# Tile 0's value products read v where it was loaded, in two halves of 64 rows; one stage's norms and copies change engines

## The chip, the cores and the metric

The kernel runs on one core of a Trainium2 chip. Its time is the device time of one launch in microseconds (us); what is shown is the median of several runs. The profile's engines are PE (TensorE, the matrix engine, with its weight loads as PEld), DVE (VectorE), ACT (ScalarE), POOL (GpSimd) and SP (SyncE, which only issues transfers here). Each engine takes its instructions in the order in which the program issued them to it; engines wait for one another through semaphores. Matrix products land in PSUM, which has eight banks of 512 fp32 columns on 128 partitions.

## What is computed

Sliding-window attention over 8 batches, 8 heads, 576 positions and 64 values a head, and then a two-layer network with the activation h cos(h) on all 4608 rows. `_attn_ref` and `_moe_ref` are these lines, with the constants filled in:

```python
scores = q @ k.T / 8                       # per batch and head, [576, 576]
rel = pos[:, None] - pos[None, :]
scores = where((rel >= 0) & (rel < 64), scores, -1e9)
attn = softmax(scores)
x = (attn @ v)  ->  [8 * 576, 512]         # heads side by side
h = x @ w_in                               # [4608, 2048]
out = (h * cos(h)) @ w_out                 # [4608, 512], fp32
```

## The kernel before, in words

**Attention.** A *unit* is 64 queries of one batch and one pair of heads (p = 0..3), against the at most 128 keys that they can see: their own block j of 64 keys and block j-1. The two heads of the pair lie on the two halves of the 128 partitions. Units go in groups of four (`GF`). For each group n: scores into one PSUM bank (`g_scores`), the row maxima on VectorE (`g_max`), exponentials with their row sums on ScalarE (`g_exp`, four instructions, each with a read of its accumulator), reciprocals on VectorE (`g_inv`), the product with them, called the norm here, on GpSimd or VectorE (`g_norm`, line 302), four transposes on TensorE into a bank of the rotating three named "t" (`g_trans`, line 311), and a copy out of it into `wT` on VectorE or ScalarE (`g_put`, through `copy`, line 109). `wT` has keys on its partitions: for odd j block j-1 on partitions 0 to 63 and block j on 64 to 127, for even j the other way round (`k_cols`, line 211).

**Values.** `load_v` (line 159) puts 128 rows of v of one batch into every second of eight slots: slot 2c has block 2c on its lower 64 partitions and block 2c+1 on the upper ones. Odd slots are filled by copies on the chip: `spread_v(0, 0)` copies lower halves of slots 2, 4, 6 to slots 1, 3, 5, `spread_v(0, 1)` copies upper halves of slots 0, 2, 4, 6 to slots 1, 3, 5, 7. Then slot j-1 has both blocks that unit j needs, each on the partitions on which `wT` has its keys, and one product on 128 rows per head and unit is enough (`values`, line 323: 16 products of 64 columns for a pair and a tile of 512 rows). `put_x` casts the bank to `xT`, which is what the network's first layer reads.

**The network.** Rows go in nine tiles of 512 (mt). A tile's first layer is 16 blocks (ff) of 4 products with w_in (line 351), one product for each pair of heads; a block's bank goes through a sine on ScalarE (line 519) and a product on VectorE (line 522) into `gT`; then 64 products with w_out (line 534). The attention of batch t+1 is woven into the network's tiles by a list of due times (`at`, `pump`).

**The first stage.** Tile 0 has nothing to be woven into. Its order is written out by hand in `FIRST`: each word is a step, and the order of the words is the order in which each engine gets its work. The words are: `tq.p`, `tk.p` (transposes of q, k of pair p), `pq.p.e`, `pk.p.e` (their copies out of PSUM on engine e: d VectorE, a ScalarE, p GpSimd), and, for pair p and group g of two, `s` scores, `m` maxima, `e` exponentials, `i` reciprocals, `n` norm, `w` transposes, `c` copy; `z` the two copies of `spread_v`, `v.p` values, `x.p` `put_x`; `l` the next of the loads on GpSimd's queue (w_in in three parts, batch 1's q and k rows, w_out in two parts); `tb` loads ScalarE's sine table. Products with w_in start before all four pairs are there: `h.p` issues the product of pair p for the first blocks (three of them), `hx.f` those of pairs 0 and 1 for block f, and `hl` those of pairs 2 and 3 for the first five blocks (`skew(0)` is 5). All later blocks get their four products in a row, in the tile's loop. Which bank a block uses is written in `H_FIRST`; the scores use the same five banks (`S_FIRST`), three other banks rotate as "t".

After `FIRST` GpSimd issues the last slot of batch 0's v (64 rows, block 8) and the five loads of batch 1's v.

Of the kernel before, what the change touches and what calls it, by code (L numbers as in the profile page):

```python
# [10 lines left out]
def _safe_warn(msg, *a, **kw):  # L11
# [14 lines left out]
GF = 4  # L26
# [25 lines left out]
def kernel(  # L52
# [43 lines left out]
    H_FIRST = ("O1", "X0", "X1", "S", "O0") * 3 + ("X0",)  # L96
# [69 lines left out]
    def spread_v(b, half, engine="p"):  # L166
        vt = values_of(b)
        to, of = ((vt[0:64, 1:7:2], vt[0:64, 2:8:2]), (vt[64:128, 1:8:2], vt[64:128, 0:7:2]))[half]
        if engine == "dma":
            nc.sync.dma_start(out=to, in_=of)  # L170
        else:
            copy(engine, to, of)

# [131 lines left out]

    def g_trans(n):
        w, u = st.pop(("w", n)), len(groups[n])
        if n in direct:
            st["tw", n] = t_ps = ps_t.tile([128, GF, 128], BF16, tag="t", name="tw_ps")
            for i in range(u):  # L310
                nc.tensor.transpose(t_ps[:, i], w[:, i], ident)  # L311
            return
        wT = att.tile([128, GF, 128], BF16, tag="wT", name="wT", bufs=20)
        nc.sync.dma_start(out=wT[:, 0:u], in_=w[:, 0:u].rearrange("p u c -> p (u c)"), transpose=True)
        st.update({("wT", unit): wT[:, i] for i, unit in enumerate(groups[n])})
# [18 lines left out]

    def put_x(mt, p, engine=None):
# [18 lines left out]
    def skew(mt):  # L354
        return 5 if mt < 2 else SKEW
# [6 lines left out]
    def skewed(mt, ks, n):  # L362
        for ff in range(skew(mt) if mt else SKEW):
# [110 lines left out]
    def load():  # L474
# [9 lines left out]
             "z": lambda half, engine=None: spread_v(0, half, engine),  # L484
# [3 lines left out]
             "c": lambda p, g, engine=None: g_put(2 * p + g, engine), "v": lambda p: values(0, p),  # L488
             "x": lambda p, engine=None: put_x(0, p, engine)}
# [3 lines left out]
    load_v(0, 4)  # L493
    for c in range(5):
# [82 lines left out]
```

## Time and profile before

| | before |
|---|---|
| median of 3 runs | 306.96 us (306.51 to 307.69) |
| the profiled execution's own time | 306.41 us |
| its span in the trace | 304.4 us |
| mean granted TensorE clock | 0.993 |
| busy: PE, PEld | 288.7 us (95%), 142.1 us (47%) |
| busy: DVE, ACT, POOL | 220.4 us (72%), 235.7 us (77%), 171.1 us (56%) |

How to read the lines shown below: a line of the timeline has the start in us from the span's start, the length in us, the engine, the line of the program, the operation, what it writes and reads, the shape, and how many instructions of the kind are merged in it (x4); a bracket at its end tells how long the engine stood idle before it and what ended that. The start of the next instruction of an engine can lie ahead of the end of the one before, as instructions overlap in the engine: what an instruction costs its engine is the distance from start to start. A line of the chain of waits has the start, the length and the piece of work. A line of a group has the busy time, the mean of one in ns, and the idle time before it.

### The profile page before, as it was taken

The page shows a single profiled execution, that of the slowest core. Times are in us where ns is not written, and L with a number is a line of the kernel's source. Part 1 is how long each engine was busy: PE and PEld are TensorE (multiplying, and loading weights), DVE is VectorE, ACT ScalarE, POOL GpSimd, SP SyncE. Part 2 cuts the span into 40 slices and gives each one's busy share as a digit, 9 for nine tenths or more (in the row PEclk, how much of TensorE's full clock was granted, in tenths as well). Part 3 has the DMA queues.
Part 4 walks back from the last instruction along what each step waited for, and adds up shares of the span by engine and source line. Part 5 has one row for each costly group of instructions (what it writes and reads, how often), then busy time and mean ns, then how long its engine had stood idle before and what let it go on. Part 6 is the DMA issues. An engine that isn't in the chain of part 4 may idle for free.

```text
span 304.4 us, 7847 instructions
## 1 busy us (share of the span) xinstructions
PE 288.7 (95%) x2628; PEld 142.1 (47%) x2668; DVE 220.4 (72%) x834; ACT 235.7 (77%) x786; POOL 171.1 (56%) x198
## 2 busy tenths in 40 slices
PE   3769999999999999999999999999999999999996
PEld 3544444544454445444544444444444454454443
DVE  3896889588787878787877787778778877236701
ACT  5997799967997799779987998799869986106600
POOL 8996257977774976497659665967433630000000
PEclk9989999999999999999999999999999999999999
DMA  7999999699969999999999979999994441011012
GB/s 150 181 211 207 207 155 139 105 165 191 225 114 155 225 164 132 154 201 183 138 167 208 189 106 172 157 219 123 180 172 110 87 130 62 0 72 70 0 69 71
DMA packets 165577, 43.88 MB, mean 144 GB/s; under 512 B 154720, under 2 KB 160800, under 8 KB 165536
## 3 DMA queue, kind: packets, MB, share of 16 engines
q0 software_dynamic: 99344, 18.06, 75.1%
q1 hardware_dynamic: 66048, 25.11, 40.2%
q8 instruction: 21, 0.34, 0.5%
q14 instruction: 20, 0.16, 0.2%
q10 hardware_dynamic: 144, 0.20, 0.2%
HBM read 36.70 MB, written 9.44 MB: 152 GB/s over the span
## 4 chain that ended last, share of the span: by engine, by line
PE 88%; DVE 6%; issue 2%; ACT 2%; DMA 1%; POOL 0%; DVEq 0%; POOLq 0%
PE h_ps L351 41%; PE out_ps L534 36%; PE o_ps L330 3%; PE s_ps L261 3%; DVE negm L273 1%; PE out_ps L371 1%; DMA first_f<-in_q_dram 1%; DVE w L302 1%; PE tq_ps L186 1%; DVE s L277 1%; DVE v L109 1%; PE tk_ps L186 1%; PE tw_ps L311 1%; PE s_ps L244 1%; ACT e L288 1%
## 5 line engine op out<-in xcount | busy, mean ns | idle before, releaser
L351 PE MATMUL h_ps<-xT,w_in 128*128 128x512 bf16 x556 | 127.1, 381 | 2.2 <-DVE xT L109 0.6
L534 PE MATMUL out_ps<-w_out,gT 128*128 128x512 bf16 x543 | 123.0, 379 | 1.8 <-issue 1.1
L522 DVE TENSOR_TENSOR gT<-h_ps,sin 128x512 bf16<-128x512 f32 x144 | 95.4, 688 | 33.6 <-ACT sin L519 33.4
L519 ACT ACTIVATE sin<-h_ps 128x512 f32<-128x512 f32 x144 | 82.9, 599 | 34.1 <-PE h_ps L351 32.8
L288 ACT ACTIVATE e<-s,negm 128x128 f32<-128x128 f32 x256 | 98.6, 388 | 0.3 <-DVE negm L277 0.3
L302 POOL TENSOR_TENSOR w<-e,rden 128x512 bf16<-128x512 f32 (+1 forms) x76 | 74.5, 993 | 31.5 <-DVE rden L295 29.1
L351 PEld LDWEIGHTS <-w_in 128*128 128x128 bf16 x576 | 56.0, 98 | 67.1 <-issue 2.7
L534 PEld LDWEIGHTS <-gT 128*128 128x128 bf16 x560 | 53.2, 98 | 62.4 <-issue 0.2
L277 DVE CUSTOM_DVE_ANT_0 s<-s_ps,mask 128x128 f32<-128x128 f32 x256 | 58.0, 284 | 0.1
L288 ACT ACTIVATION_READ_ACCUMULATOR e<-s,negm 128x1 f32 x256 | 48.1, 188 | 0.0
L149 POOL DMA_DIRECT2D rows<-in_q_dram x30 | 25.4, 867 | 25.9 <-DMA T<-rows 16.6
L162 POOL DMA_DIRECT2D v<-in_v_dram x35 | 29.8, 879 | 10.5 <-DMA rows<-in_k_dram 7.3
L109 ACT COPY out_sb<-out_ps 128x512 f32<-128x512 f32 (+1 forms) x18 | 10.1, 563 | 24.2 <-PE out_ps L534 18.7
L295 DVE RECIPROCAL rden<-den 128x4 f32<-128x4 f32 (+1 forms) x80 | 13.8, 172 | 19.2 <-ACT e L288 18.6
L149 POOL DMA_DIRECT2D rows<-in_k_dram x30 | 25.5, 897 | 2.2 <-DMA T<-rows 2.2
L109 DVE CAST xT<-o_ps 128x512 bf16<-128x512 f32 x27 | 17.6, 679 | 6.5 <-PE o_ps L330 6.3
L277 DVE DVE_READ_ACCUMULATOR2_ANT negm<- 128x1 f32 x256 | 21.2, 83 | 0.0
L109 DVE COPY out_sb<-out_ps 128x512 f32<-128x512 f32 x18 | 12.4, 689 | 12.0 <-PE out_ps L534 12.0
L288 ACT ACTIVATE e<-s_ps,negm 128x128 f32<-128x128 f32 x32 | 11.5, 425 | 1.6 <-DVE negm L273 1.6
L261 PE MATMUL s_ps<-T 64*64 64x128 bf16 x512 | 12.1, 221 | 0.0
L261 PEld LDWEIGHTS <-T 64*64 64x64 bf16 x512 | 8.2, 106 | 8.3 <-DVE negm L277 4.4
L330 PEld LDWEIGHTS <-v 128*64 128x64 bf16 x504 | 9.5, 112 | 4.3 <-issue 2.1
(56 smaller groups left out, 146.2 us busy)
## 6 DMA issues: line engine op xcount, KB each, us to landing
out_dram<-out_sb SPq DMA_DIRECT2D x16, 512.0 KB, 6.1
v<-in_v_dram POOLq DMA_DIRECT2D x28, 128.0 KB, 8.3
rows<-in_q_dram POOLq DMA_DIRECT2D x24, 128.0 KB, 5.2
rows<-in_k_dram POOLq DMA_DIRECT2D x24, 128.0 KB, 7.8
w_out<-in_moe_w_out_dram POOLq DMA_DIRECT2D x2, 1024.0 KB, 16.7
w_in<-in_moe_w_in_dram POOLq DMA_DIRECT2D x2, 768.0 KB, 12.4
wT<-w SPq DMA_TRANSPOSE x66, 3.9
out_dram<-out_sb SPq DMA_DIRECT2D x3, 256.0 KB, 2.0
```

The source lines that it names most:

```text
L109: {"a": nc.scalar.copy, "p": nc.gpsimd.tensor_copy}.get(engine, nc.vector.tensor_copy)(out, in_)
L149: nc.gpsimd.dma_start(out=rows(b)[lo:lo + n, slot * 512:slot * 512 + 512].rearrange("p (h d) -> p h d", h=H), in_={"q": q, "k": k}[name][b ...
L162: nc.gpsimd.dma_start(out=vt.rearrange("p (h d) -> p h d", h=H), in_=v[b, :, c * 128:c * 128 + n, :].rearrange("h p d -> p h d"))
L261: nc.tensor.matmul(out=s_ps[cross][to, u].rearrange("p (a t) -> p a t", a=2), lhsT=q_cols(b, p, j)[d], rhs=k_cols(b, p, j)[d], start=True, ...
L277: nc.vector.tensor_tensor_reduce(out=s[:, u], in0=s_ps[:, u], in1=mask[:, 2 - j % 2 if j else 0], scale=-scale if b else -1.0, scalar=BIG, ...
L288: nc.scalar.activation(e[:, u], s[:, u], AF.Exp, bias=negm[:, u:u + 1], scale=1.0 if n < n_first else -1.0, accum_out=den[:, u:u + 1])
L302: (nc.gpsimd if engine == "p" else nc.vector).tensor_tensor(out=w[:, 0:u], in0=e[:, 0:u], op=ALU.mult, in1=rden[:, 0:u].unsqueeze(2).to_br ...
L330: nc.tensor.matmul(out=o_ps[64 * h:64 * h + 64, 64 * i:64 * i + 64], lhsT=values_of(b)[:, max(j - 1, 0), 128 * p + 64 * h:128 * p + 64 * h ...
L351: nc.tensor.matmul(out=st["h", ff], lhsT=w_in_sb[:, ks, ff * 128:ff * 128 + 128], rhs=st["xT", mt][:, ks], start=start, stop=stop)
L519: nc.scalar.activation(sin, h_ps, AF.Sin, bias=math.pi / 2.0)
L522: nc.vector.tensor_tensor(out=gt[:, e], in0=h_ps, in1=sin, op=ALU.mult)
L534: nc.tensor.matmul(out=o_ps[e], lhsT=gT[ff // 2][:, ff % 2, ms * 128:ms * 128 + 128], rhs=w_out_sb[:, ff], start=ff == 0, stop=ff == n_ff - 1)
```

## The change

`spread_v` is no longer called for batch 0. Instead `values_first` reads v as it was loaded. For odd j the two blocks lie in one slot, on the partitions that `wT` wants: one product on 128 rows per head, as before. For even j the own block lies on the lower 64 partitions of slot j and block j-1 on the upper 64 of slot j-2: two products on 64 rows each, which add up in PSUM. They are issued in two steps, `va.p` (lower halves of even j, and odd j) and `vb.p` (upper halves), so a pair has 24 products and not 16. Pair 3 puts its upper halves into a bank of its own (`o2`) within `va.3`, and `put_x_last` (word `xl`) adds them: ScalarE copies `o2` to SBUF, VectorE copies the odd blocks and adds the even ones. The banks of `values_first` are X0, S and two of "t" (`O_FIRST`). One copy of 64 rows of the last slot remains for tile 1's unit of block 8 (`spread_last`, on GpSimd, behind the load of that slot).

Engines change: n.1.0 goes from VectorE to GpSimd; n.3.1 from VectorE to both, half each (`g_norm_halves`, word `nh`); pk.3, c.1.0 and c.2.0 from ScalarE to VectorE; c.3.0 and x.1 from VectorE to ScalarE; x.2 from ScalarE to VectorE. On GpSimd's queue the loads of batch 1's k rows and of w_out's first part move behind all norms. `tb` moves behind `xl`. `h.p` issues two blocks instead of three, `hx` only block 2, and `hl` the rest of three blocks instead of five.

```diff
 FIRST = (
     "tq.0 mk ck tk.0 pq.0.d pk.0.a s.0.1 tq.1 tk.1 l s.0.0 m.0.1 pq.1.d tq.2 e.0.1 pk.1.d s.1.0 pq.2.a "
-    "tk.2 s.1.1 i.0.1 tq.3 l m.0.0 m.1.0 pk.2.d n.0.1.p s.2.0 l w.0.1 tk.3 s.2.1 e.0.0 l e.1.0 m.1.1 "
-    "l i.0.0 e.1.1 pq.3.d i.1.0 m.2.0 pk.3.a e.2.0 n.0.0.p n.1.0.d z.1.p w.0.0 i.1.1 m.2.1 e.2.1 "
-    "s.3.0 s.3.1 c.0.1.d n.1.1.p c.0.0.d w.1.0 m.3.0 i.2.0 z.0.d c.1.0.a n.2.0.p w.1.1 c.1.1.d v.0 "
-    "i.2.1 v.1 n.2.1.p m.3.1 e.3.0 e.3.1 l x.0.d w.2.0 i.3.0 x.1.d h.0 c.2.0.a n.3.0.p w.2.1 h.1 hx.3 "
-    "i.3.1 n.3.1.d w.3.0 c.2.1.a w.3.1 tb v.2 c.3.0.d x.2.a c.3.1.d v.3 l x.3.d hx.4 hl "
+    "tk.2 s.1.1 i.0.1 tq.3 n.0.1.p l l m.0.0 m.1.0 pk.2.d s.2.0 w.0.1 tk.3 s.2.1 e.0.0 e.1.0 m.1.1 "
+    "i.0.0 n.0.0.p l e.1.1 pq.3.d i.1.0 n.1.0.p m.2.0 pk.3.d e.2.0 w.0.0 i.1.1 n.1.1.p m.2.1 e.2.1 "
+    "c.0.1.d s.3.0 s.3.1 i.2.0 n.2.0.p m.3.0 e.3.0 c.0.0.d w.1.0 va.0 i.2.1 n.2.1.p m.3.1 e.3.1 w.1.1 "
+    "c.1.0.d i.3.0 n.3.0.p c.1.1.d w.2.0 va.1 vb.0 w.2.1 c.2.0.d x.0.d i.3.1 nh.3.1 l l l c.2.1.a w.3.0 "
+    "c.3.0.a h.0 vb.1 x.1.a va.2 w.3.1 c.3.1.d va.3 vb.2 x.2.d h.1 hx.2 xl tb hl "
 )
...
-    H_FIRST = ("O1", "X0", "X1", "S", "O0") * 3 + ("X0",)
+    H_FIRST = ("O1", "X0", "O0", "S", "X1") * 2 + ("O1", "X0", "X1", "S", "O0", "X0")
+    O_FIRST = ("X0", "S", "t", "t")
...
+    def spread_last():
+        vt = values_of(0)
+        nc.gpsimd.tensor_copy(vt[64:128, 7], vt[64:128, 6])
...
+    def g_norm_halves(n):
+        (e, _), rden = st.pop(("e", n)), st.pop(("r", n))
+        w = att.tile([128, GF, 128], BF16, tag="w", name="w", bufs=8)
+        for engine, lo, hi in ((nc.vector, 0, 2), (nc.gpsimd, 2, 4)):
+            engine.tensor_tensor(out=w[:, lo:hi], in0=e[:, lo:hi], op=ALU.mult,
+                                 in1=rden[:, lo:hi].unsqueeze(2).to_broadcast([128, hi - lo, 128]))
+        st["w", n] = w
...
+    def values_first(p, part):
+        if part == "a":
+            st["o", 0, p] = bank(O_FIRST[p], "o_ps")
+        if p == PAIRS - 1:
+            st["o2"] = bank("X1", "o2_ps")[:, 0:MT // 2]
+        lower, upper, both = slice(0, 64), slice(64, 128), slice(0, 128)
+        parts = [(lower, j, j) for j in range(0, TU, 2)] + [(both, j - 1, j) for j in range(1, TU, 2)]
+        over = [(upper, max(j - 2, 0), j) for j in range(0, TU, 2)]
+        if part == "b":
+            parts = over
+        elif p == PAIRS - 1:
+            parts += over
+        for i, (ks, slot, j) in enumerate(parts):
+            apart = p == PAIRS - 1 and ks == upper
+            to = st["o2"][:, 32 * j:32 * j + 64] if apart else st["o", 0, p][:, 64 * j:64 * j + 64]
+            for h in range(2):
+                nc.tensor.matmul(out=to[64 * h:64 * h + 64], lhsT=vt_first(ks, slot, p, h),
+                                 rhs=st["wT", (0, p, j)][ks, 64 * h:64 * h + 64],
+                                 start=part == "a" and i == 0 or apart and j == 0, stop=True, skip_group_check=True)
...
+    def put_x_last():
+        p = PAIRS - 1
+        to, of = (x.rearrange("d (j o c) -> d o j c", o=2, c=64) for x in (st["xT", 0][:, p], st.pop(("o", 0, p))))
+        over = att.tile([128, GF, 128], F32, tag="s", name="over", bufs=4)[:, 0:2].rearrange("d a (j c) -> d (a j) c", c=64)
+        nc.scalar.copy(over, st["o2"].rearrange("d (j c) -> d j c", c=64))
+        nc.vector.tensor_copy(to[:, 1], of[:, 1])
+        nc.vector.tensor_tensor(out=to[:, 0], in0=of[:, 0], in1=over, op=ALU.add)
...
     def skew(mt):
-        return 5 if mt < 2 else SKEW
+        return 5 if mt == 1 else SKEW
...
     def skewed(mt, ks, n):
-        for ff in range(skew(mt) if mt else SKEW):
+        for ff in range(skew(mt) if mt else 2):
             first(mt, ff, ks, n == 0, n == PAIRS - 1)
...
     load_v(0, 4)
+    spread_last()
     for c in range(5):
         load_v(1, c)
```

More of the change, by code (lines that the diff above doesn't have):

```diff
@@ L332, in values, with vt_first @@
                                  rhs=wT[:, 64 * (h ^ cross):64 * (h ^ cross) + 64], start=True, stop=True, skip_group_check=True)
+    def values_first(p, part):
[17 more added lines that the diff above has]
+                                 start=part == "a" and i == 0 or apart and j == 0, stop=True, skip_group_check=True)
+    def vt_first(ks, slot, p, h):
+        return values_of(0)[ks, slot, 128 * p + 64 * h:128 * p + 64 * h + 64]
+    def put_x_last():
[5 more added lines that the diff above has]
+        nc.vector.tensor_tensor(out=to[:, 0], in0=of[:, 0], in1=over, op=ALU.add)
     def put_x(mt, p, engine=None):
@@ L483 @@
              "hx": lambda ff: [first(0, ff, ks, ks == 0, False) for ks in range(2)],
-             "z": lambda half, engine=None: spread_v(0, half, engine),
+             "nh": lambda p, g: g_norm_halves(2 * p + g),
              "s": lambda p, g: g_scores(2 * p + g, next(turn_s) % 5), "m": lambda p, g: g_max(2 * p + g),
@@ L487 @@
              "n": lambda p, g, engine: g_norm(2 * p + g, engine), "w": lambda p, g: g_trans(2 * p + g),
-             "c": lambda p, g, engine=None: g_put(2 * p + g, engine), "v": lambda p: values(0, p),
-             "x": lambda p, engine=None: put_x(0, p, engine)}
+             "c": lambda p, g, engine=None: g_put(2 * p + g, engine), "va": lambda p: values_first(p, "a"), "vb": lambda p: values_first(p, "b"),
+             "x": lambda p, engine=None: put_x(0, p, engine), "xl": put_x_last}
     for step in FIRST.split():
```

## The prediction

> **What bounds the kernel now.** I read the chain of waits first. Over the whole span it lies on TensorE, so a gain or a loss in the first stage moves the end only through the moment from which TensorE has all of its work in front of it.
>
> ```profile
> PE 88%; DVE 6%; issue 2%; ACT 2%; DMA 1%; POOL 0%; DVEq 0%; POOLq 0%
> ...
> L351 PE MATMUL h_ps<-xT,w_in 128*128 128x512 bf16 x556 | 127.1, 381 | 2.2 <-DVE xT L109 0.6
> ```
>
> The chain in order of time shows that moment:
>
> ```profile
> 17.50 1.41 DVE v L109
> ...
> 25.74 0.59 PE h_ps L351 x2
> ```
>
> At 17.5 us it still lies on VectorE, which copies v; from 25.74 on TensorE has what it needs of xT and works through the w_in products. The change lies wholly ahead of 27 us. So the question is when that point comes, and how many of tile 0's 64 w_in products (16 blocks of 4) are done by then. Before: 8 of 64 at 25.74.
>
> **Prices, engine by engine.** ScalarE, its timeline:
>
> ```profile
> 13.01 0.25 ACT L288 ACTIVATION_READ_ACCUMULATOR e<-s_ps,negm 128x1 f32 x1
> ...
> 14.37 0.28 ACT L288 ACTIVATION_READ_ACCUMULATOR e<-s_ps,negm 128x1 f32 x1
> 14.47 0.71 ACT L109 COPY T<-tk_ps 128x576 bf16<-128x576 bf16 x1
> 14.99 0.46 ACT L288 ACTIVATE e<-s_ps,negm 128x128 f32<-128x128 f32 x1
> ...
> 17.73 0.72 ACT L109 COPY wT<-tw_ps 128x512 bf16<-128x512 bf16 x1
> ...
> 21.33 0.21 ACT L288 ACTIVATION_READ_ACCUMULATOR e<-s_ps,negm 128x1 f32 x1
> ...
> 23.10 1.28 ACT L346 ACT_TABLE_LOAD   x1
> ```
>
> The exponentials of one group end 1.39 us after those of the group before (13.26 to 14.65). Between later groups stand two copies, pk.3 (14.47 to 14.99, 0.52) and c.1.0 (at 17.73, about as long), and e.3.1 waits for its maxima. The change takes both copies to VectorE. VectorE:
>
> ```profile
> 13.96 1.53 DVE L302 TENSOR_TENSOR w<-e,rden 128x512 bf16<-128x512 f32 x1
> ...
> 17.43 1.48 DVE L109 COPY v<-v 64x1536 bf16<-64x1536 bf16 x1
> 18.86 0.42 DVE L109 COPY wT<-tw_ps 128x512 bf16<-128x512 bf16 x1
> ...
> 20.54 0.66 DVE L109 CAST xT<-o_ps 128x512 bf16<-128x512 f32 x1
> ...
> 21.79 1.29 DVE L302 TENSOR_TENSOR w<-e,rden 128x512 bf16<-128x512 f32 x1
> ...
> 44.42 0.69 DVE L302 TENSOR_TENSOR w<-e,rden 128x512 bf16<-128x512 f32 x1
> ```
>
> VectorE loses the copy of v (17.43 to 18.86, 1.43) and n.1.0 (1.53); it gains pk.3 (about 0.7, as x.1 of like size takes 0.66), and c.1.0 and c.2.0 (0.42 each), less c.3.0. A norm takes 0.69 alone and 1.29 to 1.53 beside GpSimd's. GpSimd:
>
> ```profile
> 12.38 0.75 POOL L142 DMA_DIRECT2D rows<-in_q_dram  x1
> 13.11 0.76 POOL L142 DMA_DIRECT2D rows<-in_k_dram  x1
> ...
> 15.00 2.25 POOL L109 COPY v<-v 64x2048 bf16<-64x2048 bf16 x1
> ...
> 21.46 1.06 POOL L302 TENSOR_TENSOR w<-e,rden 128x512 bf16<-128x512 f32 x1
> ...
> 28.08 0.88 POOL L162 DMA_DIRECT2D v<-in_v_dram  x1 [1.38 <-DMA rows<-in_q_dram]
> 30.90 0.69 POOL L162 DMA_DIRECT2D v<-in_v_dram  x1 [1.94 <-DMA rows<-in_k_dram]
> ```
>
> It loses the 2.25 us copy, behind which n.1.1 stood, and takes n.1.0 (1.06). TensorE, its timeline and one row of its groups up to 26 us:
>
> ```profile
> 12.39 0.40 PE L311 MATMUL tw_ps<-ident,w 128*128 128x128 bf16 x4
> ...
> 18.75 0.90 PE L330 MATMUL o_ps<-wT,v 128*64 128x64 bf16 x32
> ...
> 25.74 5.32 PE L351 MATMUL h_ps<-xT,w_in 128*128 128x512 bf16 x23 [0.16 <-issue]
> 30.98 0.48 PE L186 MATMUL tq_ps<-ident,rows 64*64 64x64 bf16 x36
> 31.39 1.90 PE L351 MATMUL h_ps<-xT,w_in 128*128 128x512 bf16 x7
> ...
> 36.29 1.90 PE L351 MATMUL h_ps<-xT,w_in 128*128 128x512 bf16 x8
> 38.12 0.48 PE L186 MATMUL tk_ps<-ident,rows 64*64 64x64 bf16 x36
> ...
> 40.97 1.89 PE L534 MATMUL out_ps<-w_out,gT 128*128 128x512 bf16 x8 [0.20 <-DVE gT L522]
> ```
>
> ```profile
> L330 PE MATMUL o_ps<-wT,v 128*64 128x64 bf16 x64 | 1.9, 199 | 0.0
> ```
>
> Value products start (0.90 - 0.20)/31 = 0.023 apart, 0.20 from start to end. W_in products start (1.90 - 0.38)/7 = 0.217 apart. Around 23 us, where TensorE had half its clock (step 4), their weights are loaded 0.43 apart:
>
> ```profile
> 22.68 0.15 PEld L351 LDWEIGHTS <-w_in 128*128 128x128 bf16 x1 [0.28 <-issue]
> 23.11 0.15 PEld L351 LDWEIGHTS <-w_in 128*128 128x128 bf16 x1 [0.28 <-issue]
> ```
>
> **The change, step by step.** Up to i.1.0 (13.3 us) all stands as before, but for the order on GpSimd.
>
> 1. ScalarE. Without the two copies and the wait the last four groups end 1.39 apart after 14.65: 16.05, 17.45, 18.85, and e.3.1 at 20.25, against 21.54. VectorE keeps up: n.1.0, 1.5 us at 13.96, makes room for pk.3 (to 14.7), and the maxima of 2.1, 3.0 and 3.1 end at 15.5, 16.9 and 18.3, each before ScalarE is free for them. GpSimd keeps up too, at 1.06 a norm: n.1.0 from 14.5, n.1.1 15.6, n.2.0 16.6, n.2.1 17.7, n.3.0 19.1. This is the gain: 1.3 us.
>
> 2. Pair 1. c.1.1 stands behind i.3.0, which needs e.3.0 (18.85): it ends at 19.4 and va.1 starts at 19.45. Each pair now has 24 products instead of 16: 8 on 64 rows, 8 on 128, and 8 on the other 64, so two more changes of the rows in use. The trace has no value product on half the rows, but it has such a change: eight w_in products on 128 rows from 36.29 need 8 x 0.217 = 1.74, and the first transpose on 64 rows starts 1.83 after them, at 38.12: 0.09 for the change. Bounds for one: nothing, where the next product's rows are free, and the 0.20 of a whole product. I take 0.10, next to that row; no gain is possible, since the products are added, not taken away. va.1 leaves TensorE at 19.45 + 0.37 + 0.10 = 19.92, vb.0 ends at 19.92 + 0.10 + 0.16 + 0.20 = 20.38.
>
> 3. x.0 on VectorE: 20.42 to 21.08. Behind it, in order, stands i.3.1, ready since 20.25: it goes at 21.02, and the norm of 3.1 with it. So 0.8 of the 1.3 us is lost again. The halves: GpSimd 0.53 (half of 1.06), VectorE 0.35 if alone; at worst one after the other, 0.9. I take 0.65, the middle, since 1.29 for a whole norm beside GpSimd is also 0.6 more than alone: w.3.1 can start at 21.85.
>
> 4. TensorE's clock. These stretches stand in a table of busy times; the columns are each engine's busy time, then the granted clock:
>
> ```profile
> 13.43:16.84 3.41, 2.26 (x34) 1.35 (x34) 3.41 (x8) 3.41 (x20) 3.35 (x3) 1.00 1.22 208
> 16.84:20.25 3.41, 1.67 (x42) 1.22 (x41) 3.41 (x7) 3.23 (x18) 3.33 (x4) 1.00 1.16 211
> 20.25:23.67 3.42, 2.86 (x10) 1.42 (x11) 2.42 (x5) 2.92 (x11) 3.40 (x5) 0.50 1.17 210
> ```
>
> From 20.25 to 23.67 it had half clock, after a stretch in which it was busy for 1.67 of 3.41 us; 2.26 in the one before kept full clock. By the walk above the change has it busy about 2.0 there (va.0 with w.1.1 and w.2.0 1.25, va.1 and vb.0 0.75): between the two, and a part of it on half the rows. I take half clock again, because most of that stretch is still idle waiting, and keep the other as a rival. The Trainium skill, TensorE: Matmul & The Clock Gate, "What's actually happening", says that the clock is halved after an idle window of about 3.4 us; the 3.42 us here agree in length, but the window ahead of it was half busy, not idle. By that rule alone the stretch would go away, and the time would be that of rival (a).
>
> 5. On at half clock, in TensorE's order, with all of this queued behind h.0's wait for x.0: h.0, two products from 21.1, to 21.96; vb.1 to 22.5 (8 at 0.046, changes doubled); va.2 to 23.45; w.3.1, four transposes (0.40 at full clock), to 24.05; c.3.1 24.05 to 24.47. Full clock from 23.67: va.3, with its upper halves into a bank of its own, 24 products and three changes, 24.5 + 0.55 + 0.3 + 0.2 = 25.5; vb.2 25.7. x.2 25.75 to 26.41. Then the end of pair 3 in two operations of half the width (each between 0.33, half of the 0.66, and 0.66; I take 0.33 from start to start and 0.42 to the end, as the 512 columns of a 2-byte copy show 0.42 against 0.66): the copy from 26.35, the sum 26.68 to 27.1. Before, one cast did it. ScalarE copies the second bank by 25.95 and loads the sine table behind it, 1.28 + 0.2, to 27.4. At 23.10 nothing waited for that, and nothing does now, just: the first block's last product ends at 27.1 + 0.38.
>
> 6. Tally. At 27.1 the change has done h.0, h.1, hx.2 and one of hl: 7 of 64. Before had 8 at 25.74 and by 27.1 some 6 more (23 in 5.24): 14. Seven products of 0.217 are 1.5 us.
>
> 7. Back from this: from 25.74 to 40.97 TensorE needed 56 x 0.217 + 4 x 0.41 (36 transposes, 30.98 to 31.39) + 0.3 for scores = 14.1 us and took 15.23. Of the 1.1 lost, 5.24 - 23 x 0.217 = 0.25 lie ahead of 30.98, where five blocks were ready at once and VectorE drained them; with three instead of five that goes. Between 0 and 1.1; I take 0.3, the row. Everything else in this stage keeps its order.
>
> 8. What I cost at nothing: the copy in the last slot (64x512 of the 64x2048 that took 2.25, so 0.56) stands behind GpSimd's norms and ahead of loads that wait for earlier transfers anyway, to 28.08 and 30.90; without that cover 0.56 of load issue. The issues behind the norms (k rows, w_out's two parts, v) all shift by 1 to 9 us on GpSimd's queue; what hides that is the queue of transfers, in which the q rows ahead of them land only at 27.8 (rival c).
>
> Sum: 1.5 - 0.3 = +1.2 us. The profiled execution took 306.41 us (span 304.4 and 2.0 around it), 0.55 below the median of 306.96. So 307.6 against its own time, **308.1** against the runs.
>
> **Rivals.** (a) *The half clock goes.* Step 5 then saves 0.43 in h.0, 0.55 in 24 products, 0.2 in w.3.1, 0.2 in changes: 1.4 us, and w.3.1, at 22.3, still finds its norm done. 306.7. For it: 2.0 is nearer to 2.26 than to 1.67. Against: VectorE still sets the pace there, TensorE waits.
>
> (b) *The changes of rows cost a whole product each* (slower): seven lie on the path (va.1, vb.0, vb.1, va.2, two in va.3, vb.2), three of them at half clock. At 0.20 instead of 0.10 that is 7 x 0.1 + 3 x 0.1 = 1.0: 309.1. It gives over 0.5% from about 0.14 a change. Against: the 0.10 above. The Trainium skill, TensorEngine Tiling (Array Packing), "Key Properties", says that a change of the tiling mode drains TensorE. By that, 309.1; by the row, 308.1; the 0.09 us ahead of 38.12 are less than the 0.38 that the product before still had to run, so no whole drain shows there.
>
> (c) *The k rows of batch 1 come late* (slower). Their issue moves from 13.1 behind all norms, to 21.6. The table of transfers has
>
> ```profile
> rows<-in_q_dram POOLq DMA_DIRECT2D x1, 576.0 KB, 15.4
> rows<-in_k_dram POOLq DMA_DIRECT2D x1, 576.0 KB, 17.5
> ```
>
> and TensorE turns them from here on:
>
> ```profile
> 33.22 0.22 PE L186 MATMUL tk_ps<-ident,rows 64*64 64x64 bf16 x2
> ```
>
> If they again took 17.5 us, they would land at 39.9 and TensorE would stand from 34.4, 5.5 us: 313.6. It decides from 11 us to landing. Against: the q rows, ahead in the queue, landed at 12.38 + 15.4 = 27.8 and k at 30.6, so k moved only in the last 2.8 us; an issue at 22.4 is early enough.
>
> (d) *Faster*: full clock, changes for nothing (0.7 back) and all the 0.8 that step 7 leaves: 306.7 - 0.7 - 0.8 = 305.2. For it speaks only that each lies within its bounds.
>
> **How the numbers follow.** Forecast 0.48 (by itself 307.3 to 308.9), (a) 0.25, (b) 0.16, (c) 0.05, (d) 0.06. A measurement tells about 0.5%, 1.5 us, from no change: 305.4 to 308.5. Slower is (b), (c) and the upper quarter of the forecast, 0.12; faster is (d) and 0.03 of (a); the rest, 0.58, is the same. The range 305.8 to 309.8 holds (a) and (b) with the far bounds of their small terms (the halves of the norm 0.25 dearer, the two half-width operations 0.3 each) and leaves out (c) and (d).
>
> **What would show it.** Step 1: e.3.1's last row ends near 20.3. Step 3: i.3.1 starts behind x.0, near 21. Step 4: granted clock from 20.3 to 23.7. Step 5: c.3.1 near 24.1 and the sum of pair 3 near 27. Step 6: seven w_in products before it. The prediction is wrong if xT is whole before 26 us at half clock, if TensorE waits for k rows, or if the stage up to the first w_out product gets shorter by more than 0.5 us.

## The result, and the profile after

| | before | after |
|---|---|---|
| median of the runs | 306.59 us (10 runs, 306.0 to 307.69) | 309.03 us (10 runs, 306.4 to 309.76) |
| ratio, 95% interval | | 1.0083 (1.0062 to 1.0105) |
| profiled execution: own time, span | 306.41, 304.4 us | 307.50, 305.7 us |
| its mean granted TensorE clock | 0.993 | 0.994 |
| first transpose to first w_out product, called the stage below | 36.54 us (4.43 to 40.97) | 36.90 us (4.48 to 41.38) |

The change made the kernel slower by 0.8%: 2.4 us between the medians. Between the two profiled executions the stage grew by only 0.36 us and the span by 1.3: some 0.9 us of it came later, in code that the diff doesn't touch.

TensorE's timeline of the kernel after, in the stage:

```profile
18.63 0.25 PE L364 MATMUL o_ps<-wT,v 64*64 64x64 bf16 x4 [0.47 <-ACT e L293]
19.16 0.86 PE L364 MATMUL o_ps<-wT,v 64*64 64x64 bf16 x20 [0.27 <-DVE wT L110]
...
20.81 1.03 PE L395 MATMUL h_ps<-xT,w_in 128*128 128x512 bf16 x2
21.77 0.80 PE L364 MATMUL o_ps<-wT,v 64*64 64x64 bf16 x24
22.51 0.57 PE L324 MATMUL tw_ps<-ident,w 128*128 128x128 bf16 x4
...
23.59 0.86 PE L364 MATMUL o_ps<-wT,v 64*64 64x64 bf16 x28 [0.34 <-DVE wT L110]
24.39 1.25 PE L395 MATMUL h_ps<-xT,w_in 128*128 128x512 bf16 x4
25.91 5.55 PE L395 MATMUL h_ps<-xT,w_in 128*128 128x512 bf16 x25 [0.27 <-DVE xT L377]
...
41.38 1.89 PE L579 MATMUL out_ps<-w_out,gT 128*128 128x512 bf16 x8 [0.20 <-DVE gT L567]
```

Where before had its w_in products flowing from 25.74, after waits for the sum of pair 3 (`xT L377`) and flows from 25.91. Ahead of that moment it has begun 7 of the 64 products (two at 20.81, five in the group at 24.39: its length of 1.25 is four distances of 0.217 and the 0.38 of one product; one record is missing), against 8 before. One product fewer and 0.17 us later are 0.39 us, and the w_out products start 0.41 later. The row of 24 at 21.77 is vb.1 with va.2.

VectorE, the same stretch:

```profile
20.07 0.69 DVE L110 CAST xT<-o_ps 128x512 bf16<-128x512 f32 x1 [0.63 <-PE o_ps L364]
20.67 0.17 DVE L300 RECIPROCAL rden<-den 128x4 f32<-128x4 f32 x1
20.88 0.42 DVE L315 TENSOR_TENSOR w<-e,rden 128x256 bf16<-128x256 f32 x1
23.11 0.42 DVE L110 COPY wT<-tw_ps 128x512 bf16<-128x512 bf16 x1 [1.81 <-PE tw_ps L324]
24.50 0.69 DVE L110 CAST xT<-o_ps 128x512 bf16<-128x512 f32 x1 [0.96 <-PE o_ps L364]
...
25.44 0.41 DVE L377 TENSOR_TENSOR xT<-o_ps,over 128x256 bf16<-128x256 f32 x1
```

ScalarE and GpSimd, one fence each:

```profile
19.60 0.38 ACT L293 ACTIVATION_READ_ACCUMULATOR e<-s_ps,negm 128x1 f32 x1
```

```profile
20.92 0.85 POOL L315 TENSOR_TENSOR w<-e,rden 128x256 bf16<-128x256 f32 x1 [1.01 <-DVE rden L300]
21.72 0.81 POOL L143 DMA_DIRECT2D rows<-in_k_dram  x1
...
25.03 0.61 POOL L177 COPY v<-v 64x512 bf16<-64x512 bf16 x1
...
30.33 0.69 POOL L163 DMA_DIRECT2D v<-in_v_dram  x1 [1.25 <-DMA rows<-in_k_dram]
```

e.3.1 ends at 19.98; i.3.1 stands behind x.0 and starts at 20.67; the two halves of the norm run side by side and end at 21.77. c.3.1, at 23.11, waits for TensorE's transposes (w.3.1, 22.51), not for the norm.

The table of busy times (us of PE, PEld, DVE, ACT and POOL, then the granted clock, the DMA share and GB/s) shows where the half clock lay:

```profile
16.08:19.49 3.41, 1.69 (x40) 1.41 (x40) 2.74 (x8) 3.41 (x22) 2.86 (x4) 1.00 1.16 210
19.49:22.90 3.41, 3.41 (x54) 2.27 (x50) 1.20 (x3) 2.15 (x7) 2.40 (x4) 0.50 1.16 210
```

It has the length and the kind of place that it had before, but begins at 19.49 instead of 20.25.

The later loss lies in one place, in tile 3: from the first w_out product of tile 2 to that of tile 3 there are 31.77 us instead of 30.87, and for every other tile the two profiles agree within 0.03. TensorE's timeline of the kernel after, and of the kernel before, at the value products of that tile:

```profile
120.52 0.61 PE L343 MATMUL o_ps<-wT,v 128*64 128x64 bf16 x14
121.68 1.25 PE L343 MATMUL o_ps<-wT,v 128*64 128x64 bf16 x50 [0.54 <-DMA wT<-w]
```

```profile
120.08 1.41 PE L330 MATMUL o_ps<-wT,v 128*64 128x64 bf16 x64
```

After, the products stop 0.54 us for a transposed w, and the 64 take 2.41 us from the first start to the last end (to 122.93) instead of 1.41. The transfer lies on the chain of waits. The norms of that tile stand on GpSimd behind a load of v, which waited 2.33 us for a k transfer (before, 1.10; the norms started at 109.64 and not 111.26). The chain, and GpSimd's timeline:

```profile
118.87 3.55 DMA wT<-w
```

```profile
110.56 0.69 POOL L163 DMA_DIRECT2D v<-in_v_dram  x1 [2.33 <-DMA rows<-in_k_dram]
111.26 5.05 POOL L307 TENSOR_TENSOR w<-e,rden 128x512 bf16<-128x512 f32 x5
```

### The profile page after: what moved, and what is told of

It is laid out like the page before. It is cut to its first block, busy times and chain, and to the rows that moved or that the text cites. A ratio compares the mean times of both kernels' runs of the same rounds, so it can differ in the third digit from the quotient of the medians.

```text
span 305.7 us, 7915 instructions
## 1 busy us (share of the span) xinstructions
PE 290.0 (95%) x2661; PEld 143.5 (47%) x2700; DVE 218.5 (71%) x835; ACT 235.2 (77%) x785; POOL 171.3 (56%) x200
## 4 chain that ended last, share of the span: by engine, by line
PE 84%; ACT 5%; DVE 3%; issue 3%; DMA 2%; POOL 2%; POOLq 0%; DVEq 0%
PE h_ps L395 40%; PE out_ps L579 34%; ACT e L293 3%; PE s_ps L266 3%; PE o_ps L343 3%; POOL w L307 2%; DMA wT<-w 1%; PE out_ps L415 1%; PE tw_ps L324 1%; DMA first_f<-in_q_dram 1%; PE o_ps L364 1%; PE tq_ps L191 1%; DVE s L282 1%; PE tk_ps L191 0%; DVE gT L567 0%
## 5 line engine op out<-in xcount | busy, mean ns | idle before, releaser
L307 POOL TENSOR_TENSOR w<-e,rden 128x512 bf16<-128x512 f32 (+1 forms) x77 | 75.4, 990 | 37.8 <-DVE rden L300 34.6
```

The source lines that it names most:

```text
L307: (nc.gpsimd if engine == "p" else nc.vector).tensor_tensor(out=w[:, 0:u], in0=e[:, 0:u], op=ALU.mult, in1=rden[:, 0:u].unsqueeze(2).to_br ...
```

## The experiments

Two theories for the difference of the medians, which is larger than the difference of the profiles. T1: the number of stretches at half clock differs from launch to launch, and they cost the kernel after more. T2: the work itself (halves, second bank, three blocks begun ahead instead of five, loads dealt out anew) costs it.

**Before and after once more.** No edit: b_again is the kernel before, a_again and a_third the kernel after.

> The kernel before, once more, to see the granted clock of each of its runs. In the runs of the changed kernel the time went with the mean clock: 306.4 us at 0.999, 307.5 at 0.994, 308.4 to 309.1 at 0.989, 309.5 to 309.8 at 0.983, so about 1 us for each stretch of 3.4 us at half clock, of which there were 0 to 3. Clock theory: the kernel before has 0 or 1 such stretch in nearly every run (0.993 to 0.999), and at an equal clock the two kernels differ by under 0.6 us. Rival (the added row changes and the longer end of pair 3 cost time at any clock): its clocks spread like those of the changed kernel, and at an equal clock it is faster by 1.5 us or more.

> The changed kernel, once more, for a second profile and five more pairs of clock and time. Clock theory: again 0 to 3 half-clock stretches, 306.4 us plus about 1.05 us for each; all of them lie ahead of 30 us in the trace. A third theory (the wait of 0.54 us for a transposed wT at 121.7 us in the first profile is part of every run): the same wait stands in this profile too, and the time is 0.9 us above what the clock says; otherwise it is gone.

> The kernel after a third time, for a trace with two or three stretches at half clock. Theory (each such stretch costs about 1 us, the stretches lie in the first stage, ahead of 26 us, and follow a stretch of 3.41 us in which TensorE was busy for about half): median near 308.5; in a profile with a mean clock of 0.983 to 0.989 the stage takes 1 to 2 us more than the 36.26 of the profile without any. Rival (the stretches lie later, in the network's tiles, and the stage is as long): stage 36.3, the loss behind 41 us.

b_again took 305.86 us, ratio 1.0001 (0.9978 to 1.0023); a_again 308.33, 1.0065 (1.0038 to 1.0093); a_third 308.70, 1.0063 (1.0029 to 1.0098). Every run gives its mean clock. One stretch of 3.41 us at half clock takes 0.5 x 3.41 of 305 us from that mean, 0.0056, so the number of such stretches can be read from it. All launches of the two kernels beside this study's runs, by that number (the ten of before in the first table are left out, as only the profiled one has its clock on record):

| mean clock | stretches | before: launches, median us | after: launches, median us |
|---|---|---|---|
| 0.999 to 1.000 | 0 | 11, 305.17 | 7, 306.59 |
| 0.993 to 0.994 | 1 | 47, 306.33 | 5, 307.50 |
| 0.988 to 0.989 | 2 | 59, 306.34 | 9, 308.96 |
| 0.983 | 3 | 1, 308.16 | 10, 309.61 |
| all | | 118, 306.13 | 31, 308.82 |

After pays (309.61 - 306.59) / 3 = 1.0 us for each stretch, and a third of its launches have three; before pays 1.2 for the first and nothing for the second. T2 has its part in this table too: without any stretch after is 1.4 us slower (306.59 against 305.17), with one 1.2, with two 2.6. So the expectation ahead of b_again, that before has none or one and that the two differ by under 0.6 us at an equal clock, failed twice: 8 of its 12 launches had two. The profiles show why a stretch costs the one kernel more than the other. Busy times and clock of a_third, with two stretches:

```profile
16.62:20.03 3.41, 2.25 (x52) 1.89 (x53) 2.29 (x8) 3.35 (x20) 2.78 (x3) 1.00 1.16 209
20.03:23.45 3.42, 3.16 (x42) 1.78 (x39) 1.51 (x4) 1.66 (x3) 2.68 (x4) 0.50 1.16 211
23.45:26.86 3.41, 3.18 (x33) 1.83 (x34) 1.35 (x3) 1.86 (x3) 3.37 (x5) 0.50 1.21 207
26.86:30.27 3.41, 3.41 (x18) 1.52 (x17) 2.44 (x4) 2.65 (x5) 2.09 (x3) 1.00 1.22 207
```

and of b_again, also with two:

```profile
12.20:15.61 3.41, 1.08 (x31) 0.85 (x29) 2.88 (x7) 3.41 (x19) 3.35 (x5) 1.00 1.54 197
15.61:19.03 3.42, 3.32 (x34) 1.73 (x33) 2.65 (x5) 2.80 (x15) 3.34 (x3) 0.50 1.18 214
19.03:22.45 3.42, 2.95 (x43) 2.12 (x43) 3.01 (x8) 3.13 (x17) 3.29 (x4) 0.50 1.15 209
22.45:25.86 3.41, 3.21 (x50) 1.99 (x49) 2.15 (x4) 2.54 (x4) 3.41 (x5) 1.00 1.19 207
```

In b_again they lie from 15.61 to 22.45, mostly where the other engines set the pace, and its stage is no longer than with the one stretch of before (36.08 us against 36.54; b_warm, below, has 35.54 with none). In a_third they lie from 20.03 to 26.86, over the last pairs and the first w_in products, and its stage is 37.93 us, against 36.90 with one (after) and 36.26 in a_again, whose profile has none. No profile has three. That is T1's loss, in the stage, and not the rival's behind it; but a_third also lost more behind the stage, 265.1 us from the first w_out product to the end of the span against 264.0 in a_again.

In a_again a stretch like those that led to half clock elsewhere was followed by full clock:

```profile
15.99:19.40 3.41, 1.59 (x35) 1.20 (x32) 2.79 (x9) 3.41 (x21) 3.06 (x4) 1.00 1.16 210
19.40:22.81 3.41, 2.84 (x64) 1.90 (x64) 1.82 (x5) 2.40 (x8) 2.53 (x4) 1.00 1.16 211
```

TensorE was busy there for 1.59 of 3.41 us, less than the 1.69 ahead of the half clock in the kernel after. The half-clock stretches begin at 20.25, 19.49, 20.03 and 15.61 us in four profiles whose first transposes all start between 4.3 and 4.5. Both fit stretches that are counted by a clock of their own, at another offset in each launch; that is read from these rows, not measured by itself.

**The clock held up** (a_warm, b_warm, b_late). Products of a mask with the identity into a spare bank (`k.BANK.N`: N of 512 columns) stand where TensorE waited.

```diff
+    def warm(which, n):
+        spare = bank(which, "warm_ps")
+        for _ in range(n):
+            nc.tensor.matmul(out=spare, lhsT=ident, rhs=mask16[:, 2:6]..., start=True, stop=True)
 a_warm:
-... w.0.0 ... w.1.0 va.0 ... w.2.0 va.1 ... c.3.0.a h.0 ... w.3.1 c.3.1.d va.3
+... k.S.1 w.0.0 k.S.2 ... w.1.0 k.X1.5 va.0 ... w.2.0 k.X1.3 va.1 ... c.3.0.a k.X1.2 h.0 ... w.3.1 k.X1.2 c.3.1.d va.3
 b_warm (b_late: k.X1.5 ahead of h.0):
-... z.1.p w.0.0 ... w.1.0 m.3.0 ... x.1.d h.0
+... z.1.p k.S.4 w.0.0 ... w.1.0 k.X1.5 m.3.0 ... x.1.d k.X1.2 h.0
```

> The changed kernel with 15 more products of the identity and the mask (0.217 us each at full clock), written into banks that the next user overwrites, at five places of the first stage where TensorE waits. Nothing else is changed. Clock theory: the clock stays full in nearly all runs (0.997 or more) and the time is 306.2 to 306.8 us, against a median of 309.0. Rival (row changes and the end of pair 3): the median stays above 308 or rises by the time of the products that do not fit their gaps.

> The kernel before with 11 such products at three places where TensorE waits (ahead of the transposes of 0.0, behind those of 1.0, ahead of the first w_in product). Clock theory: 0.997 or more, and some 1 us faster than before, 305.3 to 306.0 us. Rival: no change, or slower by what does not fit.

> The kernel before with warming products (b_warm), and three more of them ahead of the first w_in product, which end the first stage about 0.5 us later, at 36.0 to 36.2 us from the first transpose to the first w_out product (b_warm 35.54, a_warm 36.21). Rival of the load order: the same wait for wT as in the changed kernel appears near 121 us and the time rises by 1 us or more. Load order: no such wait, and the time rises by 0.5 us at most.

a_warm took 306.51 us, every one of its 12 launches at full clock, ratio 1.0016 (0.9996 to 1.0037): 15 products more, and 1.8 us less than a_again beside it. b_warm took 305.77, 0.9992 (0.9968 to 1.0016), 11 of 12 at full clock. T1 holds for some 1.8 us of after's median; for before the products changed nothing that is clear of the noise (b_again, without them, 305.86). b_late took 305.42, 0.9996 (0.9969 to 1.0023); its stage wasn't lengthened as it was meant to be (35.35 us), so it doesn't test how a later stage meets the transfers. Its profiled launch took 309.58, against 305.1 to 306.1 in the other eleven: TensorE waits 2.38 us there for a transposed w, at 62 us. So such a wait can come to a kernel with the old stage as well. At full clock the median of a_warm is 0.7 above that of b_warm (their intervals overlap), and its stage 36.21 against 35.54: that is T2's part. TensorE in a_warm, its added products and the value products of vb.1 and va.2:

```profile
16.15 1.24 PE L277 MATMUL warm_ps<-mask,ident 128*128 128x512 bf16 x5
...
21.34 0.58 PE L370 MATMUL o_ps<-wT,v 64*64 64x64 bf16 x24
```

The 24 value products at 21.34 are 16 on 64 rows (upper halves, then lower ones) and 8 on 128 rows. Views of shorter windows tell them apart:

```profile
21.34 0.34 PE L370 MATMUL o_ps<-wT,v 64*64 64x64 bf16 x16
```

```profile
21.61 0.32 PE L370 MATMUL o_ps<-wT,v 128*64 128x64 bf16 x8
```

On 64 rows they start (0.34 - 0.19) / 15 = 0.010 apart, on 128 rows (0.32 - 0.20) / 7 = 0.017. From the last start on 64 rows, 21.49, to the first on 128 there are 0.12: this change of rows costs some 0.10 us. From the upper halves to the lower ones, both on 64 rows, nothing shows.

**What the parts cost, at full clock** (a_whole, b_three, a_five). a_whole is a_warm without the halves: 16 products on 128 rows for each pair, x.3 in one operation; its even blocks are multiplied with slot j as it lies, whose upper rows are another block's. b_three is b_warm with three blocks begun ahead. a_five is a_warm with five.

```diff
 a_whole:
-        parts = [(lower, j, j) for j in range(0, TU, 2)] + ...
+        parts = [(both, j, j) for j in range(0, TU, 2)] + ...        (no vb, no o2; x.3.d for xl)
 b_three, against b_warm:
-        return 5 if mt < 2 else SKEW                                 (and hx.3, hx.4 taken out)
+        return 5 if mt == 1 else SKEW
 a_five, against a_warm:
-... w.3.1 k.X1.2 c.3.1.d va.3 vb.2 x.2.d h.1 hx.2 xl tb hl
+... w.3.1 hx.3 c.3.1.d va.3 vb.2 x.2.d h.1 hx.2 xl hx.4 tb hl        (and 5 if mt < 2)
```

> a_warm with 16 products of 128 rows for each pair: even blocks read the slot of their own block on all 128 rows, so that their second half multiplies the wrong block of v; no second step, no bank apart and one cast for pair 3. What it leaves out is the correct sum of even blocks. It shows what the halves cost. The prediction has two row changes of 0.10 us and eight more products in each pair and 0.3 to 0.4 us in pair 3's end, 1.2 us on the path at full clock: 36.21 falls to about 35.0 from the first transpose to the first w_out product. But in the trace of a_warm the 24 products of vb.1 and va.2 together take 0.58 us, no more than 16 whole ones and a bit; by that the halves cost 0.3 to 0.5 us and the stage takes about 35.8.

> b_warm with three blocks of w_in products begun ahead of tile 0's last pairs instead of five (no hx.3, no hx.4, and the last step fills three blocks). If the fewer blocks are what lengthens the stage (step 6 of the prediction), it takes 0.4 to 0.7 us longer than b_warm, 35.9 to 36.2 us from the first transpose to the first w_out product, and the changed kernel's 36.21 is mostly that. If VectorE's drain of five ready blocks cost as much (step 7), it stays within 0.2 us of 35.54.

> The kernel after with the warming products, and five blocks begun ahead again instead of three: blocks 3 and 4 get their products of pairs 0 and 1 in the middle of the stage (the one in place of the warming products ahead of c.3.1, the other behind xl), so the end of the stage has two more blocks whose w_in products are ready. Theory (the copies of v and the halves cost about the same, and what is left of the stage's loss is the blocks begun ahead): from the first transpose to the first w_out product 35.5 to 35.8 us instead of 36.21, and 305.8 to 306.1 us instead of 306.5, all at full clock. Rival 1 (the number of blocks matters only where copies of v leave TensorE idle late): the stage stays within 0.2 of 36.21 and the time at 306.5. Rival 2 (blocks 3 and 4 take banks that pair 3's second bank and the sine need): new waits of TensorE on PSUM, stage over 36.4, 306.8 or more.

| all at full clock in their profiles | values of tile 0 | blocks begun ahead | stage us | median us | ratio, 95% |
|---|---|---|---|---|---|
| b_warm | copies | 5 | 35.54 | 305.77 | 0.9992 (0.9968 to 1.0016) |
| b_three | copies | 3 | 36.24 | 306.34 | 1.0016 (0.9999 to 1.0033) |
| a_warm | halves | 3 | 36.21 | 306.51 | 1.0016 (0.9996 to 1.0037) |
| a_whole | neither | 3 | 34.89 | 305.64 | 0.9994 (0.9974 to 1.0014) |
| a_five | halves | 5 | 35.26 | 305.94 | 1.0004 (0.9987 to 1.0021) |

The halves, their second bank and the two operations behind it cost 36.21 - 34.89 = 1.32 us of the stage. Where the cost arises can be seen on VectorE, in the cast x.2 of a_warm and in x.2 and x.3 of a_whole:

```profile
23.68 0.69 DVE L110 CAST xT<-o_ps 128x512 bf16<-128x512 f32 x1 [0.96 <-PE o_ps L370]
```

```profile
22.27 1.28 DVE L110 CAST xT<-o_ps 128x512 bf16<-128x512 f32 x2
```

In a_warm x.2 waits for vb.2, which stands behind va.3, and in the same way x.0 for vb.0 (20.04 us against 19.31 in a_whole). So the casts, and what stands behind them, pay for the second step. The copies that they replace, with the old dealing of norms and copies, cost 36.24 - 34.89 = 1.35. So the change of method is worth nothing either way, and what it loses of the stage at full clock is the two blocks: 0.70 us by b_three against b_warm, 0.95 by a_warm against a_five. These are stages of one profile each (a_again, at full clock without the added products, has 36.26 to a_warm's 36.21); the medians go the same way, but their intervals overlap. In a_five nothing on TensorE waits from 22.79 on:

```profile
22.27 0.38 PE L401 MATMUL h_ps<-xT,w_in 128*128 128x512 bf16 x1
22.79 0.93 PE L370 MATMUL o_ps<-wT,v 64*64 64x64 bf16 x32
23.65 6.22 PE L401 MATMUL h_ps<-xT,w_in 128*128 128x512 bf16 x27
```

**The order of the loads** (a_loads): a_warm with the k rows and w_out's first part issued where they were before.

```diff
-... n.0.0.p l e.1.1 ... n.3.0.p c.1.1.d ... nh.3.1 l l l c.2.1.a
+... n.0.0.p l l e.1.1 ... n.3.0.p l c.1.1.d ... nh.3.1 l c.2.1.a
```

> The changed kernel with the warming products (a_warm), and with the loads on GpSimd's queue where they stood before: batch 1's k rows right behind its q rows, w_out's first part behind the norm of 3.0. In all three profiles of the changed kernel so far (clock 0.994, 0.999, 1.0) TensorE waits 0.5 to 0.7 us at 121.7 us for a transposed wT, and the ninth-tile spacing of ScalarE's table loads around it is 14.7 to 14.8 us instead of 14.07; in the three of the kernel before it does not. Theory that the load order does this: the wait is gone, and the time falls by 0.6 to 0.9 us to about 305.7. Rival (it depends on when the first stage ends against the transfers of tile 2): the wait stays, the time stays at 306.5 or rises by the 0.35 us that a later norm costs.

It took 307.33 us, ratio 1.0053 (1.0032 to 1.0074), 0.8 above a_warm, with a stage of 36.40 us against 36.21. That points to the change's later issue being worth something; the intervals just overlap. The waits of its later tiles are other ones. TensorE's waits (what for, us in total, how often, the longest) in a_loads, then in a_warm:

```profile
PE s_ps L266 <- DMA T<-rows: 1.0, 1, 1.0
PE o_ps L349 <- DMA wT<-w: 0.4, 1, 0.4
```

```profile
PE o_ps L349 <- DMA wT<-w: 0.7, 1, 0.7
```

So the wait in tile 3 is not owed to the place of those two loads. Waits of 0.5 to 0.8 us in all for a transposed w stand in all profiles of the kernel after, in a_warm and in a_five, in neither of the kernel before. But a_whole, with after's loads, has none, and b_warm, b_late and b_three have small or large waits elsewhere. From the first w_out product to the end of the span, before took 263.4 us in both its profiles, after 264.3, 264.0 and 265.1, a_five 264.3, b_warm 264.8. What decides which transfer meets which wait stays open.

**Neither copies on an engine nor halves** (a_sp, a_mix). In a_sp transfers from SBUF to SBUF on SyncE's queue make the shifted halves, and all four pairs have 16 whole products; in a_mix pair 3 alone. Both start from a_five; a_sp also lets `h.p` begin three blocks and deals the banks of the first layer anew.

```diff
 a_sp, behind all four load_v(0, c), for c from 0 to 3:
+            nc.sync.dma_start(out=vt[64:128, 2 * c + 1], in_=vt[64:128, 2 * c])
+            if c:
+                nc.sync.dma_start(out=vt[0:64, 2 * c - 1], in_=vt[0:64, 2 * c])
 a_mix, behind all four (vt: the 128 columns of pair 3):
+        nc.sync.dma_start(out=vt[0:64, 1:6:2], in_=vt[0:64, 2:7:2])
+        nc.sync.dma_start(out=vt[64:128, 1:6:2], in_=vt[64:128, 0:5:2])
-... c.2.0.d x.0.d i.3.1 nh ... x.1.a va.2 ... va.3 vb.2 x.2.d h.1 hx.2 xl hx.4 tb hl
+... c.2.0.d i.3.1 x.0.d nh ... x.1.a tb va.2 ... va.3 vb.2 x.3.d x.2.a h.1 hx.2 hx.4 hl
```

> Neither the copies by GpSimd and VectorE nor the halves: the shifted halves of batch 0's v are made by seven transfers on SyncE's queue, SBUF to SBUF, each behind the load of its slot; the values are 16 products on 128 rows for each pair, with the dealing of norms and copies of the kernel after, one operation for x.3, five blocks begun ahead, and the warming products. Theory (the account closes: copies 1.35 us, halves 1.3, three blocks instead of five 0.7 of the stage): stage 34.2 to 34.6 us, time 304.6 to 305.0, below both kernels. Rival (the seven transfers land late: they queue with v's loads, and va.0 at 17 us waits for them): va.0 starts at 19 or later, stage 36 or more, 306.5 or more. In between, what the shifted halves are late by is seen in front of va.0.

> The kernel of a_five with pair 3 alone on 128 rows: two transfers on SyncE's queue, issued behind the loads of batch 0's v, copy the shifted halves of pair 3's 128 columns only, which va.3 needs at 22.8 us, some 5 us later than va.0 needed them in a_sp; so va.3 is 16 products instead of 24, x.3 one operation on VectorE, x.2 on ScalarE behind the sine table, and i.3.1 goes ahead of x.0 on VectorE. Theory (in a_five TensorE has no gap from 22.8 us on, so what is saved is the 8 products, 0.2 us, and what earlier readiness saves ahead of them, up to 0.5): stage 34.6 to 35.0 us against 35.26, time 305.2 to 305.7. Rival (the two transfers take from 14.5 us longer than 8 us, or push other loads back): TensorE waits for them ahead of va.3, stage 35.5 or more, 306.2 or more.

Both lost. a_sp took 311.72 us, ratio 1.0194 (1.0164 to 1.0224), a_mix 307.11, 1.0028 (1.0009 to 1.0047). TensorE in a_sp, then in a_mix:

```profile
17.69 0.32 PE L369 MATMUL o_ps<-wT,v 128*64 128x64 bf16 x8
19.36 0.25 PE L369 MATMUL o_ps<-wT,v 128*64 128x64 bf16 x4 [1.35 <-DMA v<-v]
21.98 0.32 PE L369 MATMUL o_ps<-wT,v 128*64 128x64 bf16 x4 [2.37 <-DMA v<-v]
```

```profile
22.33 0.59 PE L403 MATMUL h_ps<-xT,w_in 128*128 128x512 bf16 x2
22.85 0.25 PE L372 MATMUL o_ps<-wT,v 128*64 128x64 bf16 x4
23.90 0.62 PE L372 MATMUL o_ps<-wT,v 128*64 128x64 bf16 x20 [0.80 <-DMA v<-v]
```

The transfers, from the tables of issues (how many, KB each, median us from issue to landing), a_sp and a_mix:

```profile
v<-v SPq DMA_DIRECT2D x7, 64.0 KB, 5.5
```

```profile
v<-v SPq DMA_DIRECT2D x2, 48.0 KB, 7.0
```

Transfers of a quarter of the width (three slots in one, 48 KB) took no less time than those of one whole slot (64 KB), 7.0 us against 5.5, and the issue stands behind the last load of v (15.49 and 16.26 in a_mix, after 10.84 to 14.74 in a_sp). That is the rival's outcome in both. The stage of a_sp took 40.93 us, and TensorE waited 3.7 us of them for the transfers; all its six launches show a mean clock of 0.984 to 0.989, so two stretches at half clock or three are in its loss too. Without its 0.80 of waiting a_mix's stage of 36.11 would have been near a_five's, as an estimate. No kernel here is below the kernel before by more than its interval; a_five and b_warm are level with it.

## Why the prediction was right, and where it was not

The forecast was 308.1 us in a range of 305.8 to 309.8; the median was 309.03. Against the profiled execution it was 307.6 and 307.50. The range held, but the likeliest verdict, within 0.5%, did not come: the whole interval lies above 1.005. And the text named xT whole before 26 us at half clock as a sign against it: the sum of pair 3 ended at 25.85, so by its own sign the mechanism was wrong. The medians moved by +2.4 us where +1.2 was forecast, and in the two profiled executions only 0.4 came on the path that the text describes (step 6). That the number lies in the range is luck: terms erred against each other, and what was left out made up the rest.

**Step 1** held: e.3.1 ended at 19.98 (20.25 forecast). **Step 2**: vb.0 ended at 20.02 instead of 20.38, mostly because its group of 20 started at 19.16 and not 19.45, four of va.1's products having gone ahead at 18.63. **Step 3** held: i.3.1 behind x.0 at 20.67 (21.02), the norm's end at 21.77 (21.85); its halves took 0.85, not 0.65.

**Step 4** failed in its form. It took the half clock as a fixed stretch that "stays". In the profiled execution it did, with TensorE busy for 1.69 us ahead of it; over the launches there are none to three, about 1.0 us each in the kernel after. Rival (a), the half clock gone, forecast 306.7; the seven launches without it have a median of 306.59, a_warm 306.51. The forecast's own case, one stretch, measured 307.50, and two or three, which no case of mine had, 308.96 and 309.61. Those make up 19 of 31 launches and the rest of the median. The Trainium skill, TensorE: Matmul & The Clock Gate, "What's actually happening", has the halving follow an idle window of about 3.4 us; the length agrees, but here the stretches ahead of it were busy for 1.08 to 2.25 of 3.41 us. By that rule alone rival (a) would have come in every launch.

**Step 5** was mis-sized. From h.0's end, 24 products of vb.1 and va.2 at half clock were priced at 1.49 us (21.96 to 23.45) and took 0.74 (21.77 to 22.51); va.3 and vb.2 were priced at 1.2 and took 0.86 (23.59 to 24.45), four products having gone ahead at 23.01. The distance between products was wrong, not the change of rows. The 0.023 us at full clock came from a row of 32 with a stop in it (no product starts between 18.81 and 18.96); the row of 64 at 120.08 gives (1.41 - 0.20) / 63 = 0.019. And at half clock 16 products on 64 rows started 0.014 apart and the 8 on 128 rows 0.027 apart, where I took 0.046 for all. With the 0.2 that h.0 gained by step 2, that makes up the 1.25 us by which the sum of pair 3 ended sooner than the 27.1 forecast. Its last part held: from x.2's start to the end of the sum 1.35 us, 25.75 to 27.1 forecast, 24.50 to 25.85 measured. **Rival (b)**, a whole product of 0.20 us for each change, falls with the rows 21.34 and 21.61 of a_warm: a change between 64 and 128 rows costs about the 0.10 that I took, and one between the two halves of 64 rows nothing that shows. The Trainium skill, TensorEngine Tiling (Array Packing), "Key Properties", has a change of the tiling mode drain TensorE. The trace agrees in that only the change between 64 and 128 rows shows, with 0.12 us from start to start; it doesn't show an engine that has run empty, as the first product on 128 rows starts at 21.61, before the row on 64 rows ends (21.34 + 0.34 = 21.68).

**Step 6** is the term that this changed: 7 products as forecast, but at 25.91 instead of 27.1, when before had under 9 and not 14: 0.4 us instead of 1.5. At full clock the same tally is right in kind and weighs more: b_three lost 0.70 us of the stage by two blocks fewer. **Step 7**, 0.3 back because VectorE drains three blocks more evenly than five, did not come: from its last wait to the first w_out product before took 15.23 us for 56 products, after 15.47 for 57, the same 0.24 apart as the one product. **Step 8** held: 0.61 us at 25.03 with no wait behind it. **Rival (c)** did not come: the k rows, issued at 21.72, had landed by 30.33, when the load of v that waits for them started, ahead of the transposes that need them at 33.63. **Rival (d)** didn't either.

**Left out** altogether: the 0.9 us behind the stage. Everything past 41 us was taken to keep its order and its time; the order stayed, and a wait came in tile 3. That a stage that ends at another moment meets the transfers of the later tiles differently fits the profiles; the cause wasn't tested by itself and stays open. So +1.2 was forecast for the stage, and +0.36 there and some 0.9 later were measured.

## What to carry to other kernels

Where TensorE waits on other engines for a few microseconds, read the granted clock of every launch and not of the profiled one alone: the same code had none to three half-clock stretches, and 15 useless products took 1.8 us off the median. A change that frees an engine is worth what the bounding engine can do with the time: the copies and the halves cancelled within 0.03 us of the stage, and how many blocks TensorE could begin while it waited decided. Small transfers from SBUF to SBUF are no quick copies in a stage whose queues are full: 48 KB took 7.0 us where an engine's copy took 1.4 to 2.3. And a price read from a merged row holds the row's stops: look at the single starts before multiplying it.

## What the runs showed of the hardware

The clock was halved after stretches of 3.41 us in which TensorE was busy for 1.08, 1.67, 1.69 and 2.25 us, and not after one with 2.26 (before) or, at another offset, 1.59 (a_again). After stretches at half clock that read 3.16 and 3.32 busy a second one followed (a_third, b_again), after 2.86 (before), 2.95, 3.18 and 3.41 (after) it ended. So the recorded busy time doesn't settle the clock by itself: at half clock the same work reads as longer busy time (24 value products 0.80 us in after, 0.58 in a_warm at full clock), and the 2.25 holds products on 64 rows of the array. What is counted there was not measured.

Between a value product on 64 rows and one on 128 the distance from start to start was 0.12 us at full clock (a_warm at 21.61, after at 23.77 and 24.02) and 0.17 at half clock (after at 22.15); between the two halves of 64 rows no such distance shows.
